# Layer 2's first product for two token groups together, by seven half-depth block products

## The chip, the cores and the metric

The kernel runs on one core of a Trainium2 chip, in one launch. The metric is the device time of one execution in microseconds (us), as the median of several; lower is better. TensorE (PE) does the matrix products into the eight banks of PSUM, VectorE (DVE) and ScalarE (ACT) read the banks and work on SBUF, GpSimd (POOL) helps on SBUF, and SyncE (SP) issues the transfers from and to device memory.

## The reference

A linear-attention recurrence with decay gives a vector of 512 features for each of 1,536 tokens; two feed-forward layers follow, both with weights 512 x 2048 and 2048 x 512. The change lies in the second layer:

```python
def _moe_ref(x, w_in, w_out, a, b):
    h = x @ w_in
    ...
    g = P / (Q + 1e-06)
    return (g @ w_out).astype(np.float32)

def _moe2_ref(x, w_in, w_out):
    h = x @ w_in
    g = h * (1.0 / (1.0 + np.exp(-h)))
    return (g @ w_out).astype(np.float32)
```

## The kernel before

**Tiling.** The 1,536 tokens are three groups of 512 (`GT`). A group's activations lie transposed in SBUF as four blocks of 128 features by 512 tokens. Every number that goes into a product is held as two parts, a high one that the PE takes exactly and a low one (`xh` and `xl` for activations, `ih`, `il`, `oh`, `ol` for weights, `gh` and `gl` for gated values), and a product of two such numbers is three matmuls: high by high, high by low, low by high. All matmuls of both layers take a 128 x 128 stationary block and stream 512 columns.

**Steps.** The 2,048 hidden features are 16 blocks of 128, in 8 pairs `p`. `step` does one block `j` of a pair for one group: `mm_in` (line 526) is 12 matmuls (four feature blocks, three each) into bank `h0` or `h1`; in layer 2 ACT takes the tanh of half of it (line 309, `w<-h`), DVE makes (tanh+1)*h (line 324, `w<-w,h`), ACT makes `gh` from that and DVE `gl` (line 317); then `mm_out` (line 576) is four times three matmuls into the banks `acc0` to `acc3`, which gather the group's 512 output features over all 16 blocks. After the group's last block ACT copies the four banks out (line 611) and SP stores them (line 621). So a step is 24 matmuls, and layer 2 is 3 groups x 16 steps. The order of the groups is `R["g2"]`, that is 1, 0, 2.

**Weights.** `weights(u)` brings a pair's weights into a slot: they come as 64-bit numbers (`raw`), ACT and DVE turn them into 32-bit ones (`wt`, lines 309 and 324), and ACT (line 386) and POOL or DVE (line 391) part them into high and low. There are six slots (`RING` + `LATE`), so a pass over the 8 pairs loads pairs again; these come from `spill`, a copy of `wt` in device memory. POOL does the low part for uses `u` below 30, that is for the first six pairs of layer 2.

**Order.** All work is first collected as operations with their tiles (`op`), and then emitted in one order written out as a packed table of numbers (`ORDER`). Each engine runs its own operations strictly in that order. DVE, ACT, POOL and the SP queue each stand still when their next operation waits.

Of the kernel before, what the change touches and what calls it, by code (L numbers as in the profile page):

```python
# [11 lines left out]
F32 = mybir.dt.float32  # L12
# [11 lines left out]
R = {'lw': -463.92, 'T0': 689.59, 'tau0': 13.93, 'tau1': 122.19, 'c0': -129.63, 'dc': 67.51, 'conv': 39.61, 'half': 427.29, 'absl': -34.77, 'raw': 455.03, 'ret': 752.06, 'spl': -417.39, 'hi': 301.24, 'lo': 31.56, 'inn': -277.93, 'later': -32.81, 'split': -554.53, 'out': 359.39, 'evac': -363.13, 'qload': -20.08, 'scl': 238.79, 'sc': 858.37, 'am': -44.15, 'gr': 112.48, 'av': -547.62, 'bd': 198.47, 'xh': -201.14, 'xl': 110.32, 'glp': 25, 'lop1': 15, 'lop2': 30, 'scp': 0, 'ps': 17, 'ksc': 103.89, 'qa': -467.29, 'ka': 4, 'late': 20, 'mid': 4, 'pev': -317.29, 'pld': -385.01, 'cg': -489.85, 'wm': 11, 'mk': 26.43, 'ck': 21.3, 'g2': (1, 0, 2), 'ch0': 269.21, 'ch1': -102.81, 'ch2': 64.3, 'ch3': 22.33, 'ch4': -52.46, 'ch5': 5.42, 'ch6': -78.23, 'ch7': 237.84, 'ch8': 90.06, 'ch9': -61.88, 'ch10': -106.39, 'ch11': -212.52, 'ru0': 218.22, 'lu0': -107.8, 'ru1': 40.68, 'lu1': -106.06, 'ru2': 91.09, 'lu2': 146.01, 'ru3': -37.17, 'lu3': -39.51, 'rhalf': 125.38}  # L24
# [18 lines left out]
    'XfIW!?Ual5(ML+msVNPmqLfsEN>V;5Mg1u^<)u7SjjGTmdQYFJDpjW%RGMnibNWJGsTS3yI`o2)@IV?sgQzZjqro(UlJZa*M#HHLeV~{0o$66}',
    'sz4K|EH$M1RE{RoBpN{@X%tPNWSpF*(RBJjsrVQDq^UH6X3}U%!DA>TH=_M?kkar0O3kxqHXWiPbdknV0~$|9X%7AVpXkGMnJ&>4x<=P22j}Fu',
    'bd2WFamvM4=?2{-;uCa|(()<F&3|Y<MdWcbffmwfLS|M@$G0dF3;(4kY@D9YP-J$_zzZcK|KNFYoAU4-ipl}sr5GHO^YT4fL<{Hwoul(~mhy7}',
    '4#CklIzOa}9Fk*kD2~l>xFBcZ&>V*6OI(h}`S>3_q6c)Jif~a5$A!2xSK`WCg{yIOULXlL0{7*xoQT77Vb07|xfmDcMbd`bat$uQS-2#(<5HZJ',
    'YjSBW!|gd6_v8NDfje?7ZmhHAv^3RD+?nUd0Itn-xC?jX#WIKob2pwV1Nn^9<?LLK&&d+GC|6`WSKxA-kmK_Zp1>1%A-CYN+=$C_cOJ@<cnS~W',
    'sXUx}@MPZ1O}Rdg;AuRa7xOZ1%uV>LwB$v+oR{!OUdmf|1-IfEyp3n_C|=3UxB<`NhTMz$@OjzF+j%yx;^w@ASMwU4!$-L%_vSG?n#b`x-pSW_',
    'EYIbovWs`~F+R?F_!RHu6MUNY@mjtrCwU!TlN)@C&+vXe%jfte-{zM*pBM0YzQgDFE+60v99lN<20q9e`5wRG*L*=P@_l~CZ}<UU;)nc*-}74z',
    'D<3$Fgp*}L`dc1zc=^arID$l!PyCtV$|1hYNBA&5<@9ouuW=-aCz0inB#_JUg`-G9`6E%~uf&%m@|6?GH%=-UC4(fEWD-qOSyJm?PN#wVlPg?M',  # L50
    'p7D3iB+(_aWRpUYMPf)+DIz~PxxC;%98;ci3MnjUG`kd&98z3dNGeNF0Zl16MI?lzk`j_$OG+vE$4w=+#FAfJMXE{$MJ+AWq=w{@no>sMNLooF',
    'sim1zmynWMYDsM=E3A2>g_M&z(p*|eOKBr*MFpg;w3d3(PE6X%Z$`;4c_p26mwYl(Do8~sF9oE&^pqabM|w$L2_+q*ftdD|QL<brNh4_@jisSv',
    ')YjTr`$>Q4C}YI6lcZJA0Wwxb%QzV*<7K6+kghsGCdwKaB&%eS43^chR(48P=`7vkx^$5)x=Yr{WEmpew7X7`Cc0bJOIzI|Q)RDY(tWZ)_RBOm',
    'ARDEbZjzgFLk>z$-7IZ1i_X<Ma#wE2a2X*(<)sXhnKDZb$rjlz(<RUuvQ>7-E4eN6^`5+z`*K*?=@DtJZ{&d-m1ELgA4*GoD<7nzhSU(6RgcR%',
# [11 lines left out]
    'ujXyNiMR8nKG55HGw<Ndy|q{Ns@~E^`Dkz9t-Pam_D<f#2l-$h<3oI`kMq7hz=!&5ALb){gpc>BzQl+79G~m+e5ud(Wxm#zd+1=D&+tjU&4VCB',
    'Fu_;&dY|mme5P;r4ZheH`VQadi+q8v@-@EN_xlz<;hTM>@ALz{%Mbb?Kk4Cu!yZ03<za%5LDFElPxL9CE|}%dEkf|nQU@u5y}s4=_$EK*`~0Y1',
# [63 lines left out]
def retention_two_mlps(  # L131
# [538 lines left out]
    for u, (l, g, p) in enumerate(use_order):  # L670
        if u in loads:
            weights(u)
# [64 lines left out]
```

## Time and profile before

| | |
|---|---|
| median of 3 runs | 593.6 us (593.54 to 593.75) |
| the profiled execution | 591.33 us, with a span of 589.5 us from first to last instruction |
| PE, busy share of the span | 97%, 2,950 matmuls |
| DVE | 71%, 646 operations |
| ACT | 67%, 690 operations |
| POOL | 23%, 104 operations |
| granted clock of the PE, mean | 0.997 |
| moved by the transfers | 70.02 MB |

A share is a mean over stages that differ: attention and layer 1 come first and use DVE and ACT heavily, layer 2 starts at about 320 us and uses them less from pass to pass. Matmuls overlap: each is shown 389 ns long, but the next starts sooner, so a busy PE is read together with the distance from start to start.

### The profile page before, as it was taken

The page shows a single profiled execution, that of the slowest core. Times are in us where ns is not written, and L with a number is a line of the kernel's source. Part 1 is how long each engine was busy: PE and PEld are TensorE (multiplying, and loading weights), DVE is VectorE, ACT ScalarE, POOL GpSimd, SP SyncE. Part 2 cuts the span into 40 slices and gives each one's busy share as a digit, 9 for nine tenths or more (in the row PEclk, how much of TensorE's full clock was granted, in tenths as well). Part 3 has the DMA queues.
Part 4 walks back from the last instruction along what each step waited for, and adds up shares of the span by engine and source line. Part 5 has one row for each costly group of instructions (what it writes and reads, how often), then busy time and mean ns, then how long its engine had stood idle before and what let it go on. Part 6 is the DMA issues. An engine that isn't in the chain of part 4 may idle for free.

```text
span 589.5 us, 8100 instructions
## 1 busy us (share of the span) xinstructions
PE 574.0 (97%) x2950; PEld 474.0 (80%) x2950; DVE 417.5 (71%) x646; ACT 394.2 (67%) x690; POOL 132.9 (23%) x104
## 2 busy tenths in 40 slices
PE   6969999999999999999999999999999999999997
PEld 5858787888888888888888888878888888888885
DVE  2899999999899999999999977765332213233320
ACT  7887788999999887787999887764522312424212
POOL 0554674464435200000114364300000000000000
PEclk9998999999999999999999999999999999999999
DMA  8996855543122201302226565462320000130001
GB/s 327 339 370 239 303 192 162 180 125 117 62 81 81 73 1 36 126 18 91 76 68 214 179 212 152 156 217 84 108 89 1 1 1 18 54 123 3 0 1 72
DMA packets 33368, 70.02 MB, mean 119 GB/s; under 512 B 3632, under 2 KB 3632, under 8 KB 33328
## 3 DMA queue, kind: packets, MB, share of 16 engines
q1 hardware_dynamic: 33328, 69.51, 35.1%
q8 instruction: 23, 0.38, 0.3%
q14 instruction: 17, 0.14, 0.1%
HBM read 56.91 MB, written 12.58 MB: 118 GB/s over the span
## 4 chain that ended last, share of the span: by engine, by line
PE 91%; DMA 4%; DVE 2%; ACT 1%; issue 1%; SPq 0%; ACTq 0%
PE acc L576 43%; PE h L526 43%; DMA kT<-in_kt_dram 2%; PE a L490 2%; PE a L435 2%; PE a L480 1%; DVE wt L324 1%; DMA raw<-in_moe_w_out_dram 1%; DMA qT<-in_qt_dram 1%; PE a L468 1%; SPq L343 0%; ACT raw L309 0%; DVE am L317 0%; DVE w L324 0%; PE h L468 0%
## 5 line engine op out<-in xcount | busy, mean ns | idle before, releaser
L526 PE MATMUL h<-xh,ih 128*128 128x512 f32 x384 | 150.2, 391 | 0.1
L526 PE MATMUL h<-xh,il 128*128 128x512 f32 x384 | 149.5, 389 | 0.0
L526 PE MATMUL h<-xl,ih 128*128 128x512 f32 x384 | 149.4, 389 | 0.0
L324 DVE SCALAR_TENSOR_TENSOR w<-w,h 128x512 f32<-128x512 f32 x48 | 32.6, 684 | 78.4 <-ACT w L309 78.2
L526 PEld LDWEIGHTS h<-xh,ih 128*128 128x128 f32 x384 | 72.1, 188 | 16.1 <-DVE s L324 0.6
L526 PEld LDWEIGHTS h<-xh,il 128*128 128x128 f32 x384 | 72.1, 188 | 15.0
L526 PEld LDWEIGHTS h<-xl,ih 128*128 128x128 f32 x384 | 72.1, 188 | 14.8
L309 ACT ACTIVATE w<-h 128x512 f32<-128x512 f32 x48 | 28.1, 593 | 78.7 <-PE h L526 74.2
L576 PE MATMUL acc<-gh,oh 128*128 128x512 f32 x192 | 75.9, 395 | 0.0
L576 PE MATMUL acc<-gh,ol 128*128 128x512 f32 x192 | 74.8, 390 | 0.0
L576 PE MATMUL acc<-gl,oh 128*128 128x512 f32 x192 | 74.8, 390 | 0.0
L576 PE MATMUL acc<-oh,gh 128*128 128x512 f32 x192 | 74.7, 389 | 0.0
L576 PE MATMUL acc<-ol,gh 128*128 128x512 f32 x192 | 74.7, 389 | 0.0
L576 PE MATMUL acc<-oh,gl 128*128 128x512 f32 x192 | 74.7, 389 | 0.0
L317 DVE TENSOR_TENSOR gl<-w,gh 128x512 fp32r<-128x512 f32 x48 | 34.0, 715 | 44.1 <-ACT gh L309 44.1
L391 POOL TENSOR_TENSOR ol<-wt,oh 128x512 fp32r<-128x512 f32 x28 | 38.6, 1389 | 105.6 <-ACT oh L386 94.4
L309 ACT ACTIVATE gh<-w 128x512 fp32r<-128x512 f32 x48 | 29.8, 629 | 46.7 <-PE acc L576 31.6
L324 DVE SCALAR_TENSOR_TENSOR wt<-wt,raw 128x512 int32<-128x512 int32 x64 | 45.0, 707 | 12.0 <-ACT raw L309 7.2
L391 POOL TENSOR_TENSOR il<-wt,ih 128x512 fp32r<-128x512 f32 x28 | 39.5, 1419 | 51.3 <-ACT ih L386 34.2
L309 ACT ACTIVATE raw<-raw,par 128x512 int32<-128x512 uint32 x64 | 48.1, 758 | 1.5 <-DMA raw<-in_moe_w_in_dram 0.8
L324 DVE SCALAR_TENSOR_TENSOR s<-s,par,h 128x512 f32<-128x512 f32 x65 | 48.2, 744 | 1.0
L317 POOL TENSOR_TENSOR gl<-s,gh 128x512 fp32r<-128x512 f32 x26 | 35.2, 1353 | 59.4 <-ACT gh L309 37.7
(88 smaller groups left out, 960.2 us busy)
## 6 DMA issues: line engine op xcount, KB each, us to landing
raw<-in_moe_w_out_dram SPq DMA_DIRECT2D x32, 512.0 KB, 3.7
raw<-in_moe_w_in_dram SPq DMA_DIRECT2D x32, 512.0 KB, 4.6
spill<-wt SPq DMA_DIRECT2D x32, 256.0 KB, 4.6
wt<-spill SPq DMA_DIRECT2D x32, 256.0 KB, 3.0
qT<-in_qt_dram SPq DMA_DIRECT2D x12, 256.0 KB, 5.7
kT<-in_kt_dram SPq DMA_DIRECT2D x12, 256.0 KB, 5.7
vn<-in_v_dram SPq DMA_DIRECT2D x12, 256.0 KB, 6.0
kn<-in_k_dram SPq DMA_DIRECT2D x10, 256.0 KB, 5.6
```

What stands on the lines that cost most here:

```text
L309: lambda: nc.scalar.activation(out=out_, in_=in_, func=func, **kw),
L317: op(eng, dur, rank, lambda: e.tensor_tensor(out=out_, in0=in0, in1=in1, op=alu), reads, writes, port)
L324: lambda: nc.vector.scalar_tensor_tensor(out=out_, in0=in0, scalar=scalar, in1=in1, op0=op0, op1=op1),
L391: e.tensor_tensor(out=sl.t[nm + "l"][:, us], in0=wt.t, in1=sl.t[nm + "h"][:, us].bitcast(F32), op=ALU.subtract)
L435: nc.tensor.matmul(heads(sb_[j].t)[:, hp, :], kT.t[js, hp, :], qT.t[js, hp, :], start=True, stop=True)
L468: nc.tensor.matmul(st.t[j * D : (j + 1) * D, hp * D : (hp + 1) * D], kn.t[:, 2 * hp + j, :], vn.t[:, 2 * hp + j, :], start=(hp == 0), stop ...
L480: nc.tensor.matmul(heads(xo.t)[j * D : (j + 1) * D, hp, :], vn.t[:, 2 * hp + j, :], heads(am[j].t)[:, hp, :], start=(hp == 0), stop=not mo ...
L490: nc.tensor.matmul(heads(xo.t)[:, hp, :], old.t[:, hp, :], qT.t[:, hp, :], start=False, stop=True, skip_group_check=True,)
L526: nc.tensor.matmul(h.t, sl.t[w][:, ws], x[g].t[:, c, :], start=(n == 0), stop=(n == 3 * KD - 1))
L576: nc.tensor.matmul(a.t, a1, a2, start=(first and n == 0), stop=(last and n == 2))
```

## The change

Layer 2 keeps its pass over group 1 (`g1`). The other two groups, 0 (`ga`) and 2 (`gb`), are then taken together, pair by pair from 7 to 0. For one pair, the two hidden blocks and the two groups make a 2 x 2 block product whose depth of four feature blocks is cut into two halves: by plain block arithmetic that is eight products of half the depth (6 matmuls each), and here seven, after Winograd's form of Strassen's scheme. It needs sums of activation blocks (`x_sums`, once, into the two late slots, which layer 2 therefore has no more for weights), sums of weight blocks (`joint`, per pair, into the place of group 1's activations, `xh[1]` and `xl[1]`), and sums of products (`plus`). Of the two gated values per group, those of `ga` go on to the second product at once; those of `gb` are stored to device memory (`gates`), since the four `acc` banks are taken, and come back in a last pass (`remaining`) that does only second products, pairs 0 to 7. Layer 2 now runs with four slots: pairs 3 to 0 are loaded again in the joint pass, and the output half of pairs 4 to 7 in the last pass. The table `ORDER` is new; it is the same as before up to the middle of layer 1.

```diff
-            runs = [(g, range(NPR) if n % 2 == 0 else range(NPR - 1, -1, -1)) for n, g in enumerate(R["g2"])]
+            g1, ga, gb = R["g2"]
+            runs = [(g1, range(NPR)), ((ga, gb), range(NPR - 1, -1, -1)), ((gb,), range(NPR))]
...
+        if l == 1 and use_order[i - 1][0] == 0:
+            free = [r for r in free if r < RING]
+            resident = {key: r for key, r in resident.items() if r < RING}
...
+    def x_sums(rank):
...
+        for c in range(2):
+            chain(0, c, (of(xh[gb], c), of(xh[ga], c)), ((*of(xl[gb], c), add), (*of(xl[ga], c), sub)))
+        for c in range(2):
+            t1 = full[0, c]
+            chain(1, c, (of(xh[gb], 2 + c), (lambda t1=t1: t1.t, [t1])), ((*of(xl[gb], 2 + c), add),))
+        for c in range(2):
+            t2 = full[1, c]
+            chain(3, c, (of(xh[ga], 2 + c), (lambda t2=t2: t2.t, [t2])), ((*of(xl[ga], 2 + c), add),))
+        for c in range(2):
+            chain(2, c, (of(xh[gb], 2 + c), of(xh[gb], c)), ((*of(xl[gb], 2 + c), add), (*of(xl[gb], c), sub)))
+
+    def joint(u, p, first, last):
...
+                dma(now - R["ret"] + half, 0.66, wt.t, kept.t, [kept], [wt])
+                if u in loads:
+                    parted(u, 1, sl, "io"[half], un, wt, now - R["conv"] + R["half"] * half + un)
...
+        tt("dve", rk, s1, a21, a22, ALU.add, wu, [tmp[0]], n=GT // 2)
+        tt("dve", rk, s2, s1, a11, ALU.subtract, [wu[0]], [tmp[0]], n=GT // 2)
+        tt("dve", rk, s3, a11, a21, ALU.subtract, [wu[0]], [tmp[1]], n=GT // 2)
+        tt("dve", rk, s4, a12, s2, ALU.subtract, [wu[1], tmp[0]], [tmp[1]], n=GT // 2)
+        for r in range(2):
+            k = 2 * q + r
+            act(rk, wh.t[:, k, :], tmp[r].t, AF.Copy, [tmp[r]], wh.cells[k])
+            tt("dve", rk, wl.t[:, k, :], tmp[r].t, wh.t[:, k, :].bitcast(F32), ALU.subtract, [tmp[r], *wh.cells[k]], wl.cells[k])
...
+        def plus(to, b_, x):
+            tt("dve", now, to.t, b_.t, x.t, ALU.add, [b_, x], [to], port=False)
+
+        product(b0_, block(0, 0), x_of(ga, 0), True)
+        act(now, c12.t, b0_.t, AF.Copy, [b0_], [c12], True)
+        product(b1_, wsum(1), xsum(1), True)
+        plus(c21, b1_, c12)
+        product(b0_, block(1, 0), x_of(ga, 1), False)
+        product(b1_, wsum(0), xsum(0), False)
+        plus(c22, b1_, c12)
+        product(b2_, wsum(2), xsum(2), True)
+        plus(c22, b2_, c22)
+        product(b1_, wsum(3), x_of(gb, 1), False)
+        plus(c12, b1_, c12)
+        product(b2_, block(1, 1), xsum(3), False)
+        plus(c21, b2_, c21)
...
+            act(now, w.t, h.t, AF.Tanh, [h], [w], psum_h, scale=0.5)
+            to = w if psum_h else h
+            stt(now, to.t, w.t, 1.0, h.t, ALU.add, ALU.mult, [w, h], [to], port=not psum_h)
+            if mine:
+                second(now, ga, sl, j, to, first and j == 0, last and j == 1)
+            else:
+                dma(now + R["spl"], 0.66, gates[2 * p + j].t, to.t, [to], [gates[2 * p + j]])
+
+    def remaining(u, p, first, last):
+        for j in range(2):
+            now = at_step[2 * u + j]
+            gv_ = temp()
+            dma(now - R["ret"], 0.66, gv_.t, gates[2 * p + j].t, [gates[2 * p + j]], [gv_])
+            second(now, gb, sl, j, gv_, first and j == 0, last and j == 1)
```

A `product` is six matmuls (line 767 of the changed kernel). `b0_`, `b1_`, `b2_` are three of the four banks `a0`, `a1`, `h0`, `h1`, which rotate from pair to pair. `second` makes `gh` and `gl` and does the 12 matmuls of the second product (line 604).

What the table moves is shown at three places. In all rows a name's last number is its buffer.

**PE, a turn on a bank.** Before, in the pass over group 0 of layer 2 (the end of one `mm_in`, two quarters of an `mm_out`, the start of the next `mm_in`):

```order
L526 MATMUL h_155<-xh_66,ih_72 128x512
L526 MATMUL h_155<-xl_69,ih_72 128x512
L526 MATMUL h_155<-xh_66,il_73 128x512
L576 MATMUL acc_152<-oh_74,gh_145 128x512 [waits Activation_49]
L576 MATMUL acc_152<-ol_75,gh_145 128x512
L576 MATMUL acc_152<-oh_74,gl_148 128x512 [waits DVE_49]
L576 MATMUL acc_151<-oh_74,gh_145 128x512
L576 MATMUL acc_151<-ol_75,gh_145 128x512
L576 MATMUL acc_151<-oh_74,gl_148 128x512
L526 MATMUL h_156<-xh_66,ih_72 128x512 [waits DVE_49]
```

and now, in the joint pass (the end of one product into bank `a_181`, two quarters of a second product, the start of the next product into the same bank):

```order
L767 MATMUL a_181<-oh_1334,xh_67 128x512
L767 MATMUL a_181<-ol_1335,xh_67 128x512
L767 MATMUL a_181<-oh_1334,xl_70 128x512
L604 MATMUL acc_183<-oh_82,gh_176 128x512
L604 MATMUL acc_183<-ol_83,gh_176 128x512
L604 MATMUL acc_183<-oh_82,gl_179 128x512
L604 MATMUL acc_184<-oh_82,gh_176 128x512 [waits Activation_49]
L604 MATMUL acc_184<-ol_83,gh_176 128x512
L604 MATMUL acc_184<-oh_82,gl_179 128x512
L767 MATMUL a_181<-ih_1332,xh_67 128x512 [waits DVE_49]
```

Before, the next product goes to the other bank. Now it goes to the bank that DVE has to read (`plus`) between the two, with six matmuls in between. Of the 37 `plus` operations that a product on the same bank follows, 7 have six matmuls in between, 5 have nine and the others twelve or more.

**DVE, the pass over group 1 of layer 2.** Before (lines 324 and 391 are weights being turned and parted):

```order
L324 SCALAR_TENSOR_TENSOR wt_131<-raw_124,wt_131 128x512
L324 SCALAR_TENSOR_TENSOR w_135<-w_135,h_156 128x512
L324 SCALAR_TENSOR_TENSOR wt_128<-wt_128,raw_126 128x512
L391 TENSOR_TENSOR ol_79<-wt_131,oh_78 128x512
L324 SCALAR_TENSOR_TENSOR wt_128<-raw_126,wt_128 128x512
L324 SCALAR_TENSOR_TENSOR w_134<-w_134,h_155 128x512
```

and now (line 344 is line 324 of before, 416 is 391, and 658 is a sum of activations):

```order
L344 SCALAR_TENSOR_TENSOR wt_161<-raw_156,wt_161 128x512
L416 TENSOR_TENSOR il_81<-wt_160,ih_80 128x512
L658 TENSOR_TENSOR s_0_168<-s_0_168,xl_71 128x512
L337 TENSOR_TENSOR gl_178<-w_166,gh_175 128x512
L416 TENSOR_TENSOR ol_87<-wt_163,oh_86 128x512
L344 SCALAR_TENSOR_TENSOR w_167<-w_167,h_188 128x512
L416 TENSOR_TENSOR il_81<-wt_161,ih_80 128x512
L416 TENSOR_TENSOR ol_87<-wt_159,oh_86 128x512
L658 TENSOR_TENSOR ol_1335<-s_0_168,oh_1334 128x512
L658 TENSOR_TENSOR r_172<-xh_68 128x512
```

From the first (tanh+1)*h of layer 2 up to the 17th, DVE has 96 operations before and 122 now; 22 of these are of line 658 (28 in all), and in PE's order this stretch now holds 405 matmuls.

**SP, gated values out and back.** There is no such place before. Now, at the end of the joint pass (`gate_136` and `gate_137` are those of pair 0):

```order
L363 DMA gate_137<-s_0_168 128x512 [waits DMAHW1_49,DVE_49]
L363 DMA wt_160<-spill_126 128x512 [waits DMAHW2_49]
L363 DMA gate_136<-u_0_164 128x512
L363 DMA s_2_170<-gate_137 128x512 [waits DMAHW7_49,DMAHW4_49,DMAHW1_49]
L363 DMA r_171<-gate_138 128x512 [waits DMAHW5_49,Activation_49]
L363 DMA s_1_169<-gate_136 128x512 [waits DMAHW6_49,DMAHW3_49]
```

A value is loaded again two or three places after it is stored, and SP stands until the store has landed. In PE's order 72 matmuls stand between the last product that goes into `gate_136` and the first that reads it as `gh`. SP has 64 transfers of 256 KB more than before.

## Rows read from the trace of the kernel before

**Rows 1.** The page: busy time and instructions of the engines, and its chain by engine.

```profile
PE 574.0 (97%) x2950; PEld 474.0 (80%) x2950; DVE 417.5 (71%) x646; ACT 394.2 (67%) x690; POOL 132.9 (23%) x104
...
PE 91%; DMA 4%; DVE 2%; ACT 1%; issue 1%; SPq 0%; ACTq 0%
```

**Rows 2.** The page, groups of layer products: instructions, busy, mean ns, idle time before them.

```profile
L526 PE MATMUL h<-xh,ih 128*128 128x512 f32 x384 | 150.2, 391 | 0.1
...
L526 PEld LDWEIGHTS h<-xh,ih 128*128 128x128 f32 x384 | 72.1, 188 | 16.1 <-DVE s L324 0.6
...
L576 PE MATMUL acc<-gh,oh 128*128 128x512 f32 x192 | 75.9, 395 | 0.0
```

**Rows 3.** The chain in order of time, layer 2: start us, length us, what.

```profile
453.43 5.44 PE h L526 x24
...
560.87 5.44 PE acc L576 x24
...
573.11 12.25 PE acc L576 x54
```

**Rows 4.** Busy time by stretch: layer 1 (two rows), then the three passes of layer 2.

```profile
core 0: us, PE busy (x) PEld busy (x) DVE busy (x) ACT busy (x) POOL busy (x), PEclk, DMA share, GB/s
...
100.00:200.00 100.00, 100.00 (x482) 82.23 (x481) 94.61 (x142) 95.24 (x162) 47.57 (x36) 1.00 0.30 98
200.00:280.00 80.00, 80.00 (x354) 66.02 (x353) 78.61 (x126) 64.03 (x108) 1.29 (x1) 1.00 0.19 61
...
320.00:408.00 88.00, 87.88 (x388) 72.46 (x387) 67.62 (x98) 64.57 (x113) 27.14 (x18) 1.00 0.54 175
408.00:500.00 92.00, 92.00 (x408) 76.20 (x407) 28.88 (x45) 26.98 (x47) 0.00 (x0) 1.00 0.11 35
500.00:585.00 85.00, 85.00 (x377) 70.37 (x375) 24.80 (x38) 25.16 (x45) 0.00 (x0) 1.00 0.10 35
```

**Rows 5.** Groups of DVE and POOL from 318 to 408 us, the pass over group 1.

```profile
L324 DVE SCALAR_TENSOR_TENSOR wt<-raw,wt 128x512 int32<-128x512 int32 x25 | 20.2, 806 | 0.6
L317 DVE TENSOR_TENSOR gl<-w,gh 128x512 fp32r<-128x512 f32 x16 | 12.2, 764 | 4.3 <-ACT gh L309 4.3
L324 DVE SCALAR_TENSOR_TENSOR w<-w,h 128x512 f32<-128x512 f32 x16 | 10.9, 680 | 1.8 <-ACT w L309 1.7
...
L391 POOL TENSOR_TENSOR il<-wt,ih 128x512 fp32r<-128x512 f32 x8 | 12.3, 1551 | 16.4 <-ACT ih L386 12.7 <-DVE gl L317 3.7
```

**Rows 6.** Tile bd, a DVE operation on 256 columns: ns min/median/max, first and last start.

```profile
L317 DVE TENSOR_TENSOR bd<-a,bd x12: 405/422/429, 31.4 to 95.8; 64x256 f32<-64x256 f32 x12
```

**Rows 7.** The timeline around one gated value of layer 2: start us, length us, what.

```profile
439.44 0.39 PE L526 MATMUL h<-xh,il 128*128 128x512 f32 x1
...
439.86 0.60 ACT L309 ACTIVATE w<-h 128x512 f32<-128x512 f32 x1 [3.60 <-PE h L526]
...
440.49 1.29 DVE L324 SCALAR_TENSOR_TENSOR w<-w,h 128x512 f32<-128x512 f32 x2 [3.50 <-ACT w L309]
```

**Rows 8.** The page, groups of layer 2 on DVE and ACT.

```profile
L317 DVE TENSOR_TENSOR gl<-w,gh 128x512 fp32r<-128x512 f32 x48 | 34.0, 715 | 44.1 <-ACT gh L309 44.1
...
L309 ACT ACTIVATE gh<-w 128x512 fp32r<-128x512 f32 x48 | 29.8, 629 | 46.7 <-PE acc L576 31.6
```

**Rows 9.** The page, transfers: operation, count, KB each, median us from issue to landing.

```profile
spill<-wt SPq DMA_DIRECT2D x32, 256.0 KB, 4.6
wt<-spill SPq DMA_DIRECT2D x32, 256.0 KB, 3.0
```

More of the change, by code (lines that the diff above doesn't have):

```diff
@@ L66 @@
[L66 to L70 removed]
+    'c-jrr1EOF_3;@8SJ9?u(wr$(CZQHhO+qP}nwr!icb%+WeG=zZ=I1Ld1Ar6Ft*Z>d@!ozMz1sTDChfoj+B105717{&3goXH!020ADNC?p&D(r#1',
@@ L227, in retention_two_mlps @@
         slot_of_use.append(s)
-    again = {key for key, _, old in loads.values() if old}
+    again = {(key, h) for i, (key, _, old) in loads.items() if old for h in range(2) if use_order[i][1] != (gb,) or h}
+    again |= {((1, p), 0) for p in range(NPR)}
     T0 = R["T0"]
@@ L274, in retention_two_mlps @@
         (key, h, un): Buf(f"spill{key[0]}{key[1]}{h}{un}", [P, UNIT], F32, dram)
-        for key in sorted(again)
-        for h in range(2)
+        for key, h in sorted(again)
         for un in range(2)
     }
+    gates = [Buf(f"gate{f}", [P, GT], F32, dram) for f in range(NF)]
     parts = [Buf(f"part{m}", [P, GT], F32, dram) for m in range(4)]
@@ L352, in weights @@
         for half in range(2):
+            if half == 0 and use_order[u][1] == (gb,):
+                continue
             w = w_dram[l][half].bitcast(I32)
@@ L558, in step, with project @@
         tt("pool" if s <= R["glp"] else "dve", now + R["split"], gl.t, gv_.t, gh.t.bitcast(F32), ALU.subtract, [gv_, gh], [gl])
+        project(now, l, g, sl, j, gh, gl, first, last, part)
+    def project(now, l, g, sl, j, gh, gl, first, last, part):
         for m in range(4):
@@ new lines, in x_sums, with split, chain, of @@
+    def x_sums(rank):
+        sub, add = ALU.subtract, ALU.add
+        full = {}
+        def split(i, c, t):
+            sh_, nh, cs, ch = sum_part(i, c, 0)
+            sl_, nl, cs, cl = sum_part(i, c, 1)
+            op("act", 0.52, rank, lambda: nc.scalar.activation(out=sh_.t[nh][:, cs], in_=t.t, func=AF.Copy), [t], [ch])
+            lazy(
+                "dve", rank, lambda: sl_.t[nl][:, cs], lambda: t.t, lambda: sh_.t[nh][:, cs].bitcast(F32), sub, [t, ch], [cl]
+            )
+        def chain(i, c, first, terms):
+            t = temp()
+            full[i, c] = t
+            (f0, r0), (f1, r1) = first
+            lazy("dve", rank, lambda: t.t, f0, f1, sub, r0 + r1, [t])
+            for f, r, alu in terms:
+                lazy("dve", rank, lambda: t.t, lambda: t.t, f, alu, r, [t])
+            split(i, c, t)
+        def of(x, k):
+            return rows(x, k), x.cells[k]
+        for c in range(2):
[8 more added lines that the diff above has]
+            chain(2, c, (of(xh[gb], 2 + c), of(xh[gb], c)), ((*of(xl[gb], 2 + c), add), (*of(xl[gb], c), sub)))
@@ new lines, in second @@
+    def second(now, g, sl, j, gv_, first, last):
+        gh, gl = ghs(), gls()
+        act(now + R["split"], gh.t, gv_.t, AF.Copy, [gv_], [gh])
+        tt("dve", now + R["split"], gl.t, gv_.t, gh.t.bitcast(F32), ALU.subtract, [gv_, gh], [gl])
+        project(now, 1, g, sl, j, gh, gl, first, last, None)
+    def remaining(u, p, first, last):
+        sl = slots[slot_of_use[u]]
+        for j in range(2):
[3 more added lines that the diff above has]
+            second(now, gb, sl, j, gv_, first and j == 0, last and j == 1)
```

185 lines of the change are left out of this document (134 added, 51 removed).

## The prediction

> **What bounds the kernel now.** I read the page first: PE is busy 97% of the span and 91% of the chain that ended last is PE; DVE and ACT stand at 71% and 67% [rows 1]. The reader is to see that this is not a mean hiding another bound: the groups of both products show PE idle before them for 0.1 us and less in sum [rows 2]. The chain in order of time gives the price of one matmul: 24 of them in 5.44 us, and again in the last pass 54 in 12.25 us [rows 3], so 0.227 us from start to start, though each is drawn 391 to 395 ns long [rows 2]. Last, busy time by stretch shows where the other engines have room [rows 4]. In layer 1 DVE works 94.61 of 100 us and 78.61 of 80 us while PE stays at 100%; in layer 2 it works 67.62 of 88 us in the pass over group 1, then 28.88 of 92 and 24.80 of 85. So layer 2 is paced by PE alone, and DVE has some 144 us to give there. The granted clock is 1.00 in all these stretches, the level of 2.4 GHz. The change trades in this direction: fewer matmuls, more DVE work.
>
> **What it removes from PE.** Before, groups 0 and 2 need 2 x 16 first products of 12 matmuls, 384. Now 8 pairs need seven products of 6, which is 336. Second products stay 16 x 12 per group. 48 matmuls go: 48 x 0.227 = **10.9 us**. This is on the path in full, because nothing else holds PE in layer 2 [rows 2 to 4]. A matmul's weight load goes with it; that load is 188 ns [rows 2], shorter than the slot, so it adds nothing. Could a removed matmul give back less than its slot? The nearest row for a lower price is the weight load alone: 48 x 0.188 = 9.0 us. I take 0.227, the row of exactly these matmuls back to back. The Trainium skill, "TensorE: Matmul & The Clock Gate", section "Back-to-back issue gap", states about 131 ns per matmul of 512 columns in a sustained stream of weight loads and matmuls; by that the term would be 6.3 us. The trace does not agree: 54 matmuls in a row take 0.227 us each.
>
> **What it adds to the pass over group 1.** From the first gated value of layer 2 to the 17th, DVE now has 122 operations where it had 96, mostly the sums of activations, while PE has 405 matmuls there, 405 x 0.227 = 91.9 us. At this pass's own mean, 67.62 us / 98 = 0.69 us [rows 4], they take 84.2 us, 92% of the stretch. Layer 1 runs DVE at 95% and 98% without holding PE, so it can fit; what it hides behind is 7.7 us of DVE idle time, and if that cover goes, the work queued behind the sums is `gl`, which PE waits for. Lower bound: nothing. Upper bound: all 122 at the dearest common price there, 806 ns for an operation that ran beside POOL [rows 5]: 98.3 us, 6.4 us too many. A gain is excluded, as PE has no wait here to lose. The layer 1 rows are nearest in load, so I take **0.5 us**. Fewer slots, and 16 more spill stores, belong to this stretch: its transfers keep the queues busy 54% of the time [rows 4], and I see no cost beyond the same bounds.
>
> **What it adds to the joint pass.** PE has 336 matmuls of first products and 16 x 12 of second ones: 528 x 0.227 = 119.9 us. DVE, per pair: four sums of weight halves on 256 columns, two low parts, five `plus`, four gate products, two `gl`; in four pairs four low parts of weights loaded again; and 6 activation sums left over. Full-width operations: 8 x 13 + 16 + 6 = 126 at 0.69 us = 86.9 us; half-width 32 at 0.422 [rows 6] = 13.5 us. Together 100 us of 119.9, 84%. ACT has 8 copies, 32 tanh, 16 high parts of weight sums, 16 `gh`, 16 high parts of weights and the last 6 of the activation sums, 94 at about 0.63 [rows 8] = 59 us: room enough. POOL does nothing from 408 us on [rows 4], so DVE's longer operations beside POOL end.
>
> The load fits; the turns are the cost. A product into a bank must wait until `plus` has read the bank. The trace shows no such turn, so I build one from the handoffs of a gated value: ACT starts 0.42 us after the last matmul's start, DVE 0.63 us after ACT, which is ACT's 0.60 and 0.03 for the handoff [rows 7]. A turn over DVE is then 0.42 + 0.69 + 0.03 = 1.14 us after the last matmul's start, 0.91 us after its slot. Six matmuls cover 1.36 us: a margin of 0.45 us. One DVE operation ahead costs 0.60 (two in 1.29 us, less 0.69 [rows 7]); then such a turn stalls PE for 0.15 us. Seven of the 37 turns are that close: 7 x 0.15 = **1.0 us**, which I take. Lower bound nothing; upper bound two operations ahead at each of the seven, 0.75 x 7 = 5.3 us, and about 0.1 us at each of the five turns with nine matmuls, 5.8 us in all. I choose near the lower end, since DVE stands idle for a sixth of this pass.
>
> The sums of weights go into group 1's activation tiles, which are free only after that group's last first product. 63 matmuls, 14.3 us, stand in between in the order, and an ACT and a DVE operation need 1.4 us: nothing.
>
> **The last pass and the way through memory.** 192 matmuls take 43.6 us; ACT has 16 `gh` and DVE 16 `gl` and 8 low parts, a third of that. The first value back is the critical one. From the last product that goes into it: 0.42 to `plus`, then 0.72, tanh 0.63, product 0.72, store 4.6 and load 3.0 [rows 9], `gh` 0.66 and `gl` 0.72, 11.5 us, against 72 matmuls, 16.3 us. I cost it at nothing; what hides it is the second products of pairs that are still open, and if a store and a load each took 3 us more, PE would wait for about 1 us. The other values follow with the whole pass as cover. 64 more transfers of 256 KB are 17 MB in 254 us, on queues that work 10% to 11% of the time after 408 us [rows 4]. SP stands for each store before its load; behind it are loads that are due later. The end of the program, four copies and four stores after the last matmul, is unchanged.
>
> **Sum.** -10.9 + 0.5 + 1.0 = -9.4 us. The profiled execution took 591.33 us and would take 581.9. The median of the three runs is 593.6 us, 2.3 us above it; the difference carried over gives **584.2 us**.
>
> **Rivals.**
> *DVE misses the pass over group 1.* The sums and POOL's low parts of weights lie side by side there, and the rows show what that does: 806 and 764 ns for operations that take 680 ns without it [rows 5]. For it: 92% load at the mean price. Against: layer 1's 98%. It costs 3 to 6.4 us in place of 0.5; at 4.9 the time is 584.2 + 4.4 = 588.6 us.
> *The recombination paces the joint pass*, and the kernel gets slower. Two products of each pair are added onto a bank that `plus` has just read. If DVE, in its fixed order, stands at another operation's wait (a weight sum whose load is late, a gate product whose tanh is late), it comes too late for both, and a turn's 0.91 us is exposed whole: 16 x 0.91 = 14.6 us, 593.6 - 10.9 + 0.5 + 14.6 = 597.8 us. From 12 exposed turns on (10.9 / 0.91) nothing is gained. For it: five DVE operations in a chain per pair and only four banks. Against: 30 of 37 turns have nine matmuls or more of other work in between, and DVE has a sixth to spare.
> *A removed matmul gives back less than its slot.* If the slot were partly a cost of the stream that the matmuls left over go on paying, each would give back little more than its weight load, 9.0 us in all [rows 2], and the time is 584.2 + 1.9 = 586.1 us. That the price is the same in runs of 24 and of 54 [rows 3] speaks against it. By the spacing that the Trainium skill's page "TensorE: Matmul & The Clock Gate" states, the time would be 588.8 us.
> *Transfers come late all through*: SP's stands for gated values or weights delay loads in each of the 16 pair visits by 0.6 us and more, 9.6 us and no change, 593.8 us. The queues' low load speaks against it.
>
> **How the numbers follow.** My forecast, stalls of up to 3 us, 582.7 to 585.7 us: 0.71. DVE late in the pass over group 1: 0.13. Less than a slot per matmul: 0.03. Recombination: 0.08, of which 0.01 ends near no change. Late transfers: 0.05, of which 0.01 is faster. Faster by over 0.2% (1.2 us, about what a measurement of this kernel can tell from no change): 0.71 + 0.13 + 0.03 + 0.01 = 0.88; within it 0.05; slower 0.07. The first three cases hold 0.87. The range takes them in: its low end is the full 10.9 us with half a microsecond for the runs' scatter, 582.2; its high end the first pass at its bound and the turns at 1.0, 593.6 - 10.9 + 6.4 + 1.0 = 590.1.
>
> **What would show it.** Right: PE has 2,902 matmuls less any records that are missing; 0.227 us from start to start in every pass of layer 2; the joint pass takes about 121 us and the last one 44; PE's waits on DVE in layer 2 sum to 1 to 2 us; DVE is over 90% busy in the pass over group 1 and about 84% in the joint one. Wrong in size: waits of PE for `gl` or weights before the joint pass (the first rival), or for `plus` in it (the second). Wrong in kind: another distance between matmuls, or PE waiting for transfers in the last pass.

## The result and the profile after

| | before | after |
|---|---|---|
| median of 4 runs each | 593.57 us (590.82 to 593.75) | 583.96 us (582.6 to 586.2) |
| ratio after / before | | 0.9847, 95% interval 0.981 to 0.9884 |
| the profiled execution, its span | 591.33 us, 589.5 us | 583.73 us, 582.0 us |
| moved by the transfers | 70.02 MB | 86.81 MB |

Faster by 1.5%, with the median 0.2 us under the forecast of 584.2 us. But the two profiled executions differ by 7.6 us, not by the 9.4 us of the sum. Both numbers are taken apart below.

The page after, busy time of the engines and the chain by engine:

```profile
PE 565.1 (97%) x2902; PEld 463.6 (80%) x2902; DVE 485.3 (83%) x770; ACT 416.9 (72%) x730; POOL 132.2 (23%) x104
...
PE 80%; DVE 10%; DMA 4%; ACT 2%; issue 2%; SPq 1%; ACTq 0%; DVEq 0%
```

48 matmuls are gone, as forecast. PE's share is the same 97%, but its share of the chain fell from 91% [rows 1] to 80%, and DVE's rose from 2% to 10%: the chain now runs through other engines. In order of time it shows where (start us, length us, what):

```profile
264.16 2.73 PE h L551 x12
266.90 0.75 DVE s L344
...
329.23 5.61 DMA spill<-wt
336.62 0.70 DVE xl L337
337.36 3.69 PE acc L604 x15
...
380.52 1.15 PE acc L604 x5
382.43 0.96 DVE il L416
383.40 0.79 issue
384.19 1.27 DVE w L344 x2
388.62 0.70 DVE wt L344
393.05 1.73 DVE wt L344 x3
397.38 1.43 PE acc L604 x5
...
523.02 54.41 PE acc L604 x240
```

The chain leaves PE twice: from 267 to 337 us, mostly through DVE, with a store of weights near its end, and between 382 and 397 us for DVE's weights. The first piece is 70 us long and accounts for the fall from 91% to 80%, but it is no loss of 70 us: from 267 to 324 us PE worked all 57 us, and DVE 56.5 of them, as before. A chain's share says who came last, not how long anybody stood. The last row is the whole last pass and the end of the joint one: 240 matmuls in 54.41 us, 0.227 us each, the price of [rows 3] unchanged. Busy time by stretch (columns as in [rows 4]): the pass over group 1 as it was cut there, the joint pass, the last pass:

```profile
320.00:408.00 88.00, 86.50 (x377) 70.04 (x377) 77.46 (x114) 67.66 (x117) 26.86 (x19) 1.00 0.71 225
...
404.00:524.00 120.00, 119.97 (x527) 97.97 (x526) 98.73 (x173) 57.42 (x102) 0.00 (x0) 1.00 0.30 96
524.00:578.00 54.00, 54.00 (x239) 44.48 (x237) 18.12 (x28) 19.81 (x34) 0.00 (x0) 1.00 0.47 154
```

The first row against its row in [rows 4] holds most of what went wrong: 377 matmuls in the same 88 us where before had 388, so 11 x 0.227 = 2.5 us of PE time lost; DVE 77.46 us for 67.62, and the transfers at 71% and 225 GB/s for 54% and 175. The joint pass and the last one run at PE's full rate. PE's own waits in layer 2, of which before had none that the view lists:

```profile
PE h L551 <- DVE w L344: 0.4, 1, 0.4
PE h L551 <- DVE il L416: 0.4, 1, 0.4
PE acc L604 <- DVE xl L337: 0.4, 1, 0.4
PE acc L604 <- DVE ol L416: 0.3, 1, 0.3
```

They sum to 1.5 us, less than the 2.5 us, since a matmul is drawn longer than its slot (0.39 against 0.227 us) and hides the first 0.16 us of every wait. Two of the four are for parts of weights (`il`, `ol`), and two for a bank that DVE reads late: `acc`, from which it takes `xl`, the low part of layer 1's last outputs, and `h`, from which it makes a gated value. What the text below calls **lost time** is therefore worked out from the starts of the matmuls in the trace: the sum of what each distance from start to start exceeds 0.2267 us, in the first 98 us of layer 2 and in the rest. The pass over group 1 takes 80 us of these 98, up to its last first product; the start of the joint pass is the remainder.

What ACT, which makes the weights, waits for (from 320 to 420 us):

```profile
ACT gh L329 <- DVE w L344: 5.9, 5, 2.0
ACT wt L329 <- DMA spill<-wt: 3.6, 2, 3.0
...
ACT wt L329 <- DMA raw<-in_moe_w_in_dram: 2.0, 2, 1.2
```

The second row is a turn on a `wt` tile: ACT cannot write the next weights into it before the store of the last ones has landed. In the two repeats of the change this row is 1.9 and 3.6 us, and before had none. From issue to landing a store takes 4.8 us here:

```profile
spill<-wt SPq DMA_DIRECT2D x48, 256.0 KB, 4.8
wt<-spill SPq DMA_DIRECT2D x48, 256.0 KB, 2.9
```

### The profile page after: what moved, and what is told of

Read it like the earlier page. It is cut to its first block, busy times and chain, and to the rows that moved or that the text cites. A ratio compares the mean times of both kernels' runs of the same rounds, so it can differ in the third digit from the quotient of the medians.

```text
span 582.0 us, 8304 instructions
## 1 busy us (share of the span) xinstructions
PE 565.1 (97%) x2902; PEld 463.6 (80%) x2902; DVE 485.3 (83%) x770; ACT 416.9 (72%) x730; POOL 132.2 (23%) x104
## 2 busy tenths in 40 slices
DMA packets 42585, 86.81 MB, mean 149 GB/s; under 512 B 4656, under 2 KB 4656, under 8 KB 42544
## 4 chain that ended last, share of the span: by engine, by line
PE 80%; DVE 10%; DMA 4%; ACT 2%; issue 2%; SPq 1%; ACTq 0%; DVEq 0%
PE acc L604 37%; PE h L551 24%; PE h L767 7%; PE a L767 7%; DVE wt L344 2%; DMA kT<-in_kt_dram 2%; PE a L460 2%; PE a L515 2%; PE a L505 2%; DVE s L344 1%; DMA spill<-wt 1%; DVE gl L337 1%; DMA qT<-in_qt_dram 1%; DVE t L344 1%; DVE s L337 1%
## 5 line engine op out<-in xcount | busy, mean ns | idle before, releaser
L551 PE MATMUL h<-xh,ih 128*128 128x512 f32 x256 | 100.3, 392 | 0.4 <-DVE w L344 0.4
L551 PE MATMUL h<-xh,il 128*128 128x512 f32 x256 | 99.8, 390 | 0.4 <-DVE il L416 0.4
L551 PE MATMUL h<-xl,ih 128*128 128x512 f32 x256 | 99.7, 390 | 0.0
L551 PEld LDWEIGHTS h<-xh,ih 128*128 128x128 f32 x256 | 48.0, 188 | 11.4 <-issue 0.8
L551 PEld LDWEIGHTS h<-xh,il 128*128 128x128 f32 x256 | 48.0, 188 | 10.9 <-DVE il L416 0.8
L329 ACT ACTIVATE wt<-raw 128x512 f32<-128x512 f32 x64 | 42.4, 666 | 10.1 <-DMA spill<-wt 3.6
L344 DVE SCALAR_TENSOR_TENSOR wt<-raw,wt 128x512 int32<-128x512 int32 x64 | 46.2, 729 | 0.7
L329 ACT ACTIVATE s<-h,par 128x512 f32<-128x512 f32 x48 | 37.1, 772 | 10.0 <-PE h L551 4.9
L604 PEld LDWEIGHTS acc<-oh,gh 128*128 128x128 f32 x192 | 36.0, 188 | 8.6 <-DVE xl L337 0.8
L604 PEld LDWEIGHTS acc<-ol,gh 128*128 128x128 f32 x192 | 36.0, 188 | 8.4 <-DVE ol L416 1.0
```

Source lines behind the costliest of these rows:

```text
L329: lambda: nc.scalar.activation(out=out_, in_=in_, func=func, **kw),
L344: lambda: nc.vector.scalar_tensor_tensor(out=out_, in0=in0, scalar=scalar, in1=in1, op0=op0, op1=op1),
L551: nc.tensor.matmul(h.t, sl.t[w][:, ws], x[g].t[:, c, :], start=(n == 0), stop=(n == 3 * KD - 1))
L604: nc.tensor.matmul(a.t, a1, a2, start=(first and n == 0), stop=(last and n == 2))
```

## The experiments

**Theory.** A removed matmul gives back its whole slot; what is missing of the gain is lost in the pass over group 1, because DVE comes late there: it has the activation sums on top, and 16 more stores of weights keep `wt` tiles and the queue. (Before stores the weights of pairs 0, 1, 6 and 7 of layer 2, and none between 332 and 385 us; the change stores all eight pairs.) **Rivals.** A removed matmul gives back less than a slot; POOL's low parts slow DVE; the recombination (`plus`) or the gated values' way through memory costs more than forecast; the order of the table alone is to blame.

All runs in one table. "Layer 2" is from its first matmul to its last, in one profiled execution of each kernel; the ratio to before has its 95% interval. Where a kernel keeps all 1,104 matmuls of layer 2, 1,103 slots are 250.0 us; with 1,152 they are 260.9 us. Layer 2 is compared because the time ahead of it scatters with the granted clock of the first 60 us (last section).

| run | ratio to before | layer 2 us | lost, first 98 us | of it, first 16 us | of it, 16 to 80 us | lost later |
| --- | --- | --- | --- | --- | --- | --- |
| before | 1 | 261.31 | 0.51 | 0.02 | 0.48 | 0.16 |
| the change, first profile | 0.9847 (0.981 to 0.9884) | 253.81 | 3.26 | 0.69 | 2.04 | 0.77 |
| a0_change | 0.9867 (0.9839 to 0.9895) | 252.73 | 2.26 | 0.45 | 1.39 | 0.69 |
| a0_again | 0.9865 (0.9824 to 0.9906) | 254.12 | 3.64 | 0.88 | 2.29 | 0.74 |
| e1_eighth | 1.0044 (1.0023 to 1.0064) | 264.49 | 3.58 | 1.23 | 2.33 | 0.28 |
| e2_no_sums | 0.9821 (0.9787 to 0.9854) | 251.73 | 1.60 | 0.46 | 0.73 | 0.36 |
| e3_no_pool | 0.9839 (0.9797 to 0.9881) | 252.51 | 2.02 | 1.18 | 0.39 | 0.72 |
| e4_no_gates | 0.9847 (0.9796 to 0.9899) | 252.77 | 2.26 | 0.79 | 1.05 | 0.74 |
| e5_half_spills | 0.9811 (0.9776 to 0.9845) | 251.34 | 1.03 | 0.95 | 0.06 | 0.53 |
| e6_no_plus | 0.9867 (0.9815 to 0.9919) | 253.12 | 2.89 | 0.28 | 2.20 | 0.48 |
| e7_neither | 0.9843 (0.9813 to 0.9873) | 250.76 | 0.62 | 0.54 | 0.06 | 0.37 |
| e8_reordered | 0.9862 (0.9827 to 0.9896) | 252.89 | 2.97 | 0.04 | 2.77 | 0.15 |
| e9_pool_queue | 0.9914 (0.988 to 0.9949) | 255.77 | 5.18 | 0.75 | 4.07 | 0.82 |
| e10_pool_queue_all | 0.9905 (0.9876 to 0.9935) | 257.69 | 7.20 | 1.84 | 5.10 | 0.70 |

The split is by place. The loss of the first 16 us is one wait, that of the first profile at 337 us, where DVE has yet to make `xl`; that of 16 to 80 us is the rest of the pass over group 1. The edits of e1, e4 and e6 lie in the joint pass and after it, so up to 80 us these three and the three profiles of the change show the same work six times: 0.28 to 1.23 us lost at the first place and 1.05 to 2.33 at the second. A difference inside these bands is read as nothing.

The times scatter too, and much of that goes with the clock. A straight line through all 124 executions whose clock is on record, with a level of its own for each kernel, gives 0.40 us more for each 0.001 by which the mean granted clock of an execution is lower. Taken at one clock, and to within 1.0 us, e2 is 2.5 us faster than the change, e3 2.2, e5 3.1, e7 2.9 and e8 0.1; e9 is 3.2 us slower and e10 3.4.

**The change again**, beside the experiments of its batch (a0_change) and of a later one (a0_again), with no edit.

> The changed kernel as it is, timed beside the others on one chip. Theory (48 matmuls at 0.227 us less, about 3 us of new PE waits, most of them in the pass over group 1): 7 to 10 us under the kernel before, 583.5 to 586.5 us. Rival (a removed matmul gives back less than its slot): under 6 us.

> The changed kernel once more, beside the next two on one chip: 252.7 to 253.8 us for layer 2 (from its first product's first matmul to the last matmul's start), 2.3 to 3.3 us of PE waits in its first 98 us, 7 to 9 us under the kernel before.

583.3 us against 591.53 of before, and 582.72 against 592.39: 1.33% and 1.35%, about 7.9 us each time. Three expectations were narrowly missed: the first median lies 0.2 us under its 583.5 to 586.5, and the second profile's layer 2 (254.12 us) and lost time (3.64 us) lie above theirs. In the three profiles of this kernel the lost time in the first 98 us runs from 2.26 to 3.64 us.

**e1: the eighth product put back.** The first product of each pair is done twice, 48 matmuls, and all else stays.

```diff
-        def product(b_, w, x, start):
+        def product(b_, w, x, start, times=1):
...
-                for c in range(2):
+                for c in [*range(2)] * times:
...
-        product(b0_, block(0, 0), x_of(ga, 0), True)
+        product(b0_, block(0, 0), x_of(ga, 0), True, 2)
```

> The first product of each pair is done twice, so that PE has its 48 matmuls back and nothing else changes on any engine. Theory (each matmul is a whole slot on the path): 10.4 to 10.9 us slower than the changed kernel, some 3 us slower than the kernel before in the traces. Rival (less than a slot per matmul): 6 to 9 us slower. Rival (the joint pass is paced by DVE's recombination): under 5 us slower, since the added matmuls fill waits.

594.11 us against 583.3 of the change in the same batch: 10.8 us for 48 matmuls, 0.225 each. In the traces layer 2 is 10.4 to 11.8 us longer than in the three executions of the change. The Trainium skill, "TensorE: Matmul & The Clock Gate", section "Back-to-back issue gap", states about 131 ns per matmul; an estimate by that is 6.3 us for 48, and the run does not agree. The rival of 9.0 us is not excluded by the times, as the two ratios together leave some 2 us to each side, but by the traces: the distance from start to start has a median of 0.227 us in layer 2 with and without the 48 matmuls, so those left over do not pay for the ones that went. The slot is given back whole. The run also isolates the other side of the trade: with the matmuls back the kernel is 0.44% (0.23 to 0.64%) slower than before, so what the change adds costs about 2.6 us (1.4 to 3.8).

**e2: without the activation sums.** 28 operations of DVE and 8 high parts of ACT; each keeps its place as an empty operation.

```diff
-        op(eng, dur, rank, lambda: e.tensor_tensor(out=out_(), in0=in0(), in1=in1(), op=alu), reads, writes, port)
+        op(eng, dur, rank, lambda: None, reads, writes, port)
...
-            op("act", 0.52, rank, lambda: nc.scalar.activation(out=sh_.t[nh][:, cs], in_=t.t, func=AF.Copy), [t], [ch])
+            op("act", 0.52, rank, lambda: None, [t], [ch])
```

> The 28 sums of activations on DVE and their 8 high parts on ACT are left out (old contents are multiplied instead). Theory (DVE's load in the pass over group 1 makes the waits there): PE waits there fall from about 3.0 us to under 1 us, 2 to 3 us faster than the changed kernel. Rival (the waits come from POOL's low parts blocking DVE, or from the weight buffers and slots): under 1 us faster.

**e5: without the 16 stores of the weights of pairs 4 to 7**, with the copies of pairs 0 to 3 loaded in their place. These are not the 16 stores that the change adds: pairs 4 and 5 are new, pairs 6 and 7 are stored before as well, and the new ones of pairs 2 and 3 stay.

```diff
-                    dma(need - R["ret"] + half, 0.66, wt.t, kept.t, [kept], [wt])
+                    src = spill[(l, p % 4 if l else p), half, un]
+                    dma(need - R["ret"] + half, 0.66, wt.t, src.t, [kept], [wt])
...
-                    if kept:
+                    if kept and l == 1 and p >= 4:
+                        op("sync", 0.66, need + R["spl"], lambda: None, [wt], [kept])
+                    elif kept:
...
-                dma(now - R["ret"] + half, 0.66, wt.t, kept.t, [kept], [wt])
+                src = spill[(1, p % 4), half, un]
+                dma(now - R["ret"] + half, 0.66, wt.t, src.t, [kept], [wt])
```

> In layer 2 the 16 stores of the weights of pairs 4 to 7 are left out, and the copies of pairs 0 to 3 are loaded in their place. Rival to DVE's load (weight buffers held by slow stores, ACT's wait of 3.0 us on one): PE's waits in the pass over group 1 fall from 2 to 3 us to under 1 us. Theory (DVE's load and POOL): they change by less than 0.7 us.

**e7: both of these edits together.**

> The sums of activations and the stores of the weights of pairs 4 to 7 are both left out. Theory (the waits in the pass over group 1 come from these two together, DVE's load and buffers held by stores): waits there under 0.7 us, layer 2 in 250.5 to 251.2 us, the full 48 slots of 10.9 us gained. Rival (something third, such as four slots in place of six or POOL): 1 us and more remain.

The row of 320 to 408 us from each of the three, in the order e2, e5, e7:

```profile
320.00:408.00 88.00, 87.54 (x384) 71.54 (x383) 65.82 (x98) 66.38 (x115) 26.38 (x19) 1.00 0.68 224
```

```profile
320.00:408.00 88.00, 87.36 (x385) 72.01 (x384) 79.16 (x117) 69.78 (x120) 28.23 (x19) 1.00 0.57 189
```

```profile
320.00:408.00 88.00, 87.81 (x387) 72.35 (x387) 68.21 (x100) 66.23 (x114) 27.07 (x19) 1.00 0.56 180
```

PE does 384, 385 and 387 matmuls where the change does 377 and before 388. e2 takes DVE's load back to that of before and leaves the transfers at 224 GB/s; e5 does the opposite, and DVE even gets through more operations (117 for 114 of the change), since it waits less. Of the 3.05 us that the change loses on average in its first 98 us, e2 takes away 1.45, e5 2.02 and both together 2.43. e2's time fits its theory (2.1 us under the change in its batch), its waits do not, with 1.6 us left where under 1 was expected; e5 met its rival's forecast within 0.03 us, and e7 its theory's.

By place it is plainer. From 16 us on, the stores of pairs 4 to 7 account for the whole loss: without them 0.06 us is left up to 80 us, where the six profiles of the same work lose 1.05 to 2.33. Without the sums 0.73 us is left, and e7 has nothing more to take. So the two loads do not add up: either one, taken away, gives slack to the same path of the weights (load, ACT, DVE, store, tile free). The wait of the first 16 us none of the three takes away (0.46, 0.95 and 0.54 us, inside the band). It is new, as before has none, so e7's 0.62 us is not the 0.51 us that before loses, which lies 61 us into layer 2. In the chain of the first profile this wait stands behind a store and behind DVE's full load at the end of layer 1; which of them makes it is open.

**e3: without POOL's 24 low parts of layer 2.**

```diff
+            if on_pool and l == 1:
+                return
```

> POOL's 24 low parts of weights in layer 2 are left out (old contents are multiplied instead), all else stays. Theory (DVE load alone): DVE still has 114 operations from 320 to 408 us and the waits change little, under 1 us faster. Rival (POOL's operations hold up DVE's while they run, the 1.83 us operation at 382 us): the long DVE operations go, the waits fall from 3.0 to under 1 us, 2 to 3 us faster.

The waits alone look like the theory: 2.02 us lost, just under the change's band. The time does not: 580.49 us against 583.3 of the change in the same batch, 2.8 us faster, or 2.2 at one clock, as the rival forecast. The split says why. At the first place this profile happens to lose 1.18 us, near the top of the band; from 16 to 80 us it loses 0.39 us, less than without the sums. In the first profile two of the four waits, 1.36 us together, come right behind the DVE operation at 382 us that stood 1.83 us beside POOL (last section). So POOL is a third load on the same path, worth about as much as the sums. How the three share the loss cannot be said, since each alone takes away more than half of it.

**e4: without the 32 transfers of gated values.** The stores and loads become empty operations.

```diff
-                dma(now + R["spl"], 0.66, gates[2 * p + j].t, to.t, [to], [gates[2 * p + j]])
+                op("sync", 0.66, now + R["spl"], lambda: None, [to], [gates[2 * p + j]])
...
-            dma(now - R["ret"], 0.66, gv_.t, gates[2 * p + j].t, [gates[2 * p + j]], [gv_])
+            op("sync", 0.66, now - R["ret"], lambda: None, [gates[2 * p + j]], [gv_])
```

> The 16 stores of the second group's gated values and the 16 loads are left out (the last pass multiplies what its buffers hold). Theory (the way through memory is hidden): PE's waits after 416 us stay at about 0.5 us and the last pass takes the same time, within 0.5 us. Rival (the way through memory costs): the last pass gets over 1 us shorter.

0.74 us lost later, as with them (0.69 to 0.77), and the last matmuls of the program again follow without a gap. The way through memory is hidden.

**e6: without the 40 recombinations on DVE.**

```diff
-            tt("dve", now, to.t, b_.t, x.t, ALU.add, [b_, x], [to], port=False)
+            op("dve", 0.6, now, lambda: None, [b_, x], [to])
```

> The 40 recombinations (plus) on DVE are left out, so that no product waits for a bank to be read. Theory (turns are covered, 0.5 us in all): PE's waits in the joint pass fall from 0.5 us to about 0.2, the pass takes the same time within 0.5 us. Rival (recombination paces the pass): over 1 us less.

0.48 us lost later in place of 0.69 to 0.77: all 40 turns together cost some 0.2 to 0.3 us, at the edge of what one execution tells, and the edit also takes the `plus` operations off DVE.

**e8: another order for the same operations**, the table `ORDER` alone.

```diff
 ORDER = (
...
```

> The whole changed kernel with another table: between the end of layer 1 and the start of the joint pass operations are moved by a few places on each engine, so that the sums of activations stand where DVE has room and gated values, low parts and weights come a little earlier. Theory (the waits are a matter of order at a load that fits): waits in the first 98 us of layer 2 fall from 2.3 to 3.3 us to 0.3 to 1.5 us, 1 to 2.5 us faster than the changed kernel, layer 2 in 250.8 to 252.0 us. Rival (the load does not fit): the waits move to other places and stay over 2 us.

584.02 us, 0.9862: no gain, as the rival forecast. The waits moved: the one of the first 16 us went (0.04 us) and so did the later ones (0.15 us), but from 16 to 80 us 2.77 us are lost. That no order helps is not shown by one.

**e9 and e10: the stores issued on POOL's queue**, those of pairs 4 to 7 (16) and then all of layer 2 (32). They leave nothing out.

```diff
-                        dma(need + R["spl"], 0.66, kept.t, wt.t, [wt], [kept])
+                        dma(need + R["spl"], 0.66, kept.t, wt.t, [wt], [kept], swdge=(l == 1 and p >= 4))
```

(e10: `swdge=(l == 1)`.)

> The changed kernel, nothing left out, but the 16 stores of weights of pairs 4 to 7 are issued on POOL's queue instead of SP's, at the same places of the program. In the changed kernel SP's queue stands 57 us in sum, 23 times, up to 6.1 us, for weights that a store needs, between 320 and 410 us, and loads of raw weights are queued behind. Theory 'the stores cost through SP's queue': loads come earlier, PE's waits in the pass over group 1 fall from 2.3 to 3.6 us (three executions of the change) to about 1.0 us, as where the 16 stores were left out altogether: some 2 us less than the change, ratio to before about 0.982. Theory 'the stores cost through the buffer they hold until they land, and through the transfers themselves': the waits stay at 2 to 3.6 us and the ratio at 0.986. Rival: POOL stands at the stores in place of SP, its low parts come late, and the waits grow above 3.6 us.

> As the run before, but all 32 stores of layer 2's weights on POOL's queue; nothing is left out. By 'the stores cost through SP's queue' waits of about 1.0 us or less in the pass over group 1 and a ratio of 0.982 or below; by 'through the buffer they hold and the transfers themselves' 2 to 3.6 us and 0.986; if POOL's low parts come late behind the stores, more than 3.6 us and above 0.988.

The rival held: 587.37 and 587.25 us, and 5.18 and 7.20 us lost. Issues and landings of e9 from 320 to 408 us, the stores on either queue (those of SP's are the earlier ones, up to 358 us):

```profile
spill<-wt POOLq DMA_DIRECT2D x15, 256.0 KB, 2.7
spill<-wt SPq DMA_DIRECT2D x10, 256.0 KB, 5.2
```

and what POOL, ACT and PE of e9 wait for:

```profile
POOL spill L363 <- DVE wt L344: 18.5, 5, 7.7
```

```profile
ACT wt L329 <- DMA spill<-wt: 7.8, 5, 4.2
```

```profile
PE acc L604 <- DVE gl L337: 2.2, 1, 2.2
PE acc L604 <- DVE ol L416: 1.2, 1, 1.2
```

On POOL's queue a store lands 2.7 us after its issue, where the same 16 stores took a median of 4.5 to 4.7 us on SP's in the three profiles of the change. But POOL stands 18.5 us for the weights that it is to store, and what it has to do next stands with it. The tile stays held: ACT's wait for it grew from 1.9 to 3.6 us in the profiles of the change to 7.8. This fits a price that runs from DVE's last write into the tile to the landing, and not from the issue alone. It does not isolate that price: POOL's low parts came late at the same time, and what e5 gave back may also have come from SP's queue, which stood 57 us for weights to be stored, or from the transfers themselves.

## Why the prediction was right, and where it was not

- **48 x 0.227 = 10.9 us off the path:** right. 0.227 us in the last row of the chain after, and 10.8 us when the matmuls were put back (e1).
- **The pass over group 1, 0.5 us:** the step that failed. The first 98 us lost 2.3 to 3.6 us, 1.8 to 3.1 us more than before. The load was forecast well enough (DVE 88% in the row of 320 to 408 us, 92% forecast). What failed is the inference from layer 1, that a DVE at 95% and 98% there without holding PE can carry this load here, and with it the sentence that "16 more spill stores" had "no cost beyond the same bounds". The stores were looked at as a share of busy queues, 54%, and not as the 4.6 us [rows 9] for which each holds one of five `wt` tiles that ACT and DVE need for the next weights. Without the stores of pairs 4 to 7, half of them new, the loss from 16 to 80 us is gone (0.06 us, e5); without the sums, which the forecast named, 0.73 us of it is left (e2), and without POOL's low parts 0.39 (e3). A further 0.45 to 0.88 us is the wait for `xl` in the first 16 us, which no term had. The mechanism was that of the first rival (DVE late, PE waiting), at 3 us the low end of its 3 to 6.4. Its cause, POOL beside the sums, is two of the three loads; the stores it did not have.
- **The turns in the joint pass, 1.0 us:** too high. All later lost time is 0.69 to 0.77 us, 0.16 of it there before, and e6 assigns 0.2 to 0.3 us of it to the turns. DVE's load was as forecast, 98.73 of 120 us, 82% for 84%.
- **Gated values through memory, nothing:** right (e4). Their stores took a median of 2.2 us where 4.6 was reckoned, their loads 3.8 where it was 3.0.
- **The recombination as the pace, late transfers all through, less than a slot:** none of the three happened; the joint pass has 527 matmuls in 120 us, and the last 240 have no gap.
- **The sum:** with the measured terms it is -10.9 + (3.05 - 0.51) + (0.73 - 0.16) = -7.8 us in place of -9.4; layer 2 became 7.2 to 8.6 us shorter in the three executions, and the two repeats gave 7.9 us. That the forecast of the time came out within 0.2 us is luck: its sum took off 1.6 us too much, and the 593.6 us that it started from was high by about as much, as in the other comparisons before had medians of 591.5 to 593.0 us. The range, 582.2 to 590.1 us, held it, and the sign was never near its point of turning: 10.9 us against some 3.

## What to carry to other kernels

Work taken from the engine that sets the pace is worth its distance from start to start, whole, as long as nobody else takes over; look for the loss in the stretch where the helpers were already loaded most, not in the part that was rewritten. Price a store by the time for which it holds its source, from the last write to the landing, and count the tiles of that ring; here queues that were busy 54% of the time did not show it. Loads that are added to one path take from the same slack, so they are put into one sum, and leaving one of them out does not measure its share. Before a suspect is let go on one profile, compare place by place, with several profiles of the same work, and compare the times at one granted clock: the sum over e3's waits looked innocent, and its places and its time did not.

## What was not expected of the hardware

A store on POOL's queue landed in 2.7 us (e9), where the same 16 stores on SP's took 4.5 to 4.7 in the change. The Trainium skill, "DMA: Bandwidth & Descriptors", section "Issuing engine by pattern", has the path from SP as "generally faster"; by these runs it was not so for the landing of these stores, which share SP's queue with loads of 512 KB; whether that is the reason is not shown. POOL itself spends 0.54 us on an issue, and the kernel became slower.

DVE stood behind POOL (timeline of after: start us, length us):

```profile
381.15 2.56 POOL L416 TENSOR_TENSOR ol<-wt,oh 128x512 fp32r<-128x512 f32 x2 [3.03 <-PE h L551]
...
382.43 1.83 DVE L416 TENSOR_TENSOR il<-wt,ih 128x512 fp32r<-128x512 f32 x1 [1.22 <-ACT ih L411]
```

The same operation takes 686 ns in the joint pass, where POOL is idle; here it takes 1.83 us and ends only after POOL's two. The Trainium skill, "SBUF — State Buffer", section "Who interferes with whom", has a DVE instruction with two inputs in SBUF contend with a GpSimd instruction that reads SBUF, over a pair of ports that is "an exclusive lock". The row agrees: this operation has two such inputs, and it ended 0.55 us after POOL's, where a whole run behind them would have taken 0.69.

The start of an execution scatters by more than the change's open terms. In the first 60 us, TensorE's granted clock was 0.89 on the mean in a0_again and 1.00 in e7, between or at its two levels (1.2 and 2.4 GHz):

```profile
0.00:60.00 60.00, 47.68 (x464) 41.18 (x465) 40.25 (x70) 42.42 (x92) 23.01 (x24) 0.89 0.83 301
```

```profile
0.00:60.00 60.00, 48.84 (x517) 41.34 (x518) 46.43 (x79) 48.63 (x102) 26.99 (x27) 1.00 0.92 326
```

That is 53 matmuls' difference ahead of anything that was edited. The spans are 586.9 and 576.9 us, and layer 2 explains 3.4 us of the difference. What sets that clock is open.

Not tried: another `wt` tile in the ring, and reading the output halves of pairs 4 to 7 again from the 64-bit weights in the last pass, where DVE and ACT work a third of the time, in place of storing them. Whether either brings back the 2 to 3 us is open. Nor was any run made without the 16 new stores alone (pairs 2 to 5).
